# A four-layer linear-attention and PEER kernel: 83 of its 96 sets of five transposes go from TensorE to VectorE and DMAs, and every engine's order is made anew

## The chip, the cores and the metric

The kernel runs on one core of one Trainium2 chip. The metric is device time in microseconds (us) of one execution; lower is better. Before the change three runs took 755.93, 756.91 and 757.05 us, median 756.91 us. All arithmetic is fp32 or built from pairs of the rounded type fp32r, so that products keep nearly fp32 precision.

## The reference, cut to what matters

Two layers, each a linear-attention block A and a product-key expert block B, both with a layer norm in front and a residual behind. 2048 tokens, D = 576, 32 heads of 18.

```python
def A(x, wqkv, wo):                       # H = 32 heads, 18 wide
    q, k, v = split_heads(x @ wqkv)
    phi = lambda t: where(t > 0, t + 1, exp(t)) + 1e-6
    pq, pk = phi(q), phi(k)
    kv = einsum("bhsd,bhse->bhde", pk, v)  # over all 2048 tokens
    z = pk.sum(tokens)
    o = (pq @ kv) / (pq . z + 1e-6)
    return o @ wo

def B(x, w_q, k1, k2, u, v):              # 64 experts = 8 x 8
    q1, q2 = halves(x @ w_q)              # 32 heads, 128 wide each
    i1, i2 = argmax(q1 @ k1.T), argmax(q2 @ k2.T)
    e = i1 * 8 + i2                       # one expert per head
    act = gelu(x . u[e])                  # softmax over one score is 1
    return sum over heads of act * v[e]

x = x + A(layernorm(x));  x = x + B(layernorm(x))
x = x + A(layernorm(x));  x = x + B(layernorm(x))
```

## The kernel before, in words

The 2048 tokens are 16 tiles of 128. For every tile and layer there are three points at which a tile with tokens on its partitions has to become the stationary operand of a product, with channels on its partitions: the normalized input of attention (kind f), the attention output before `wo` (kind o) and the normalized input of the experts (kind b). That is 3 kinds x 16 tiles x 2 layers = 96 sets. Each set is a 128 x 640 tile (576 channels, padded to five blocks of 128). `transposed` (line 190) makes it: five TensorE transposes by the identity into a PSUM tile `pt`; ScalarE copies PSUM to the high part `thi`, rounded to fp32r (line 102); VectorE subtracts it from PSUM for the low part `tlo` (line 103). Products then take 28 matmuls of 288 columns: high by high, high by low, low by high (line 212 for k, v and q; line 402 for `wo`), or 14 of 512 columns for the expert scores (line 433). The small expert-count tile `cg` (128 x 128) is transposed with the kind-b set, where both are ready together, and gets one high and one low copy with it.

The stages run over tiles. In the front of a layer every tile gets its norm, kind f, k and v, and its part of the state `kva` (line 283), which needs all 16 tiles before the layer's back can begin: `state_mask` (VectorE, lines 305 to 308), `state_sum` (the sums `zb`), and five `state_fold` products that multiply the state into `wo`. In the back a tile gets `num` (GpSimd multiplies pq by `zb`, line 371; VectorE sums, inverts and scales, lines 374 to 379), kind o, `ppo`, a residual (line 391), the norm, kind b, the scores, the selection (VectorE, lines 461 to 498), the expert output `po` and the second residual. The front of layer 1 is interleaved with the back of layer 0. The q products of layer 1 for tiles 0 to 12 come late, from high and low parts that `keep` stores to DRAM and `rl` loads into the space of the weights for k and v. While layer 0 begins, 64 slices of `w_q` are folded with the keys (line 550).

The order is written out: each piece (k0.13 is the k product of layer 0, tile 13) is a generator whose steps are played in a listed order, and `in_order` chains the instructions of TensorE, ScalarE, VectorE and GpSimd in that order. All DMAs go through one queue on SyncE (SP). Each DMA waits on SP for its source or its buffer, and everything behind it on SP waits too. The order of SP is left to the framework. Tiles of normalized rows (`y`) have 3 buffers, stationary pairs 4, PSUM tiles 4.

## Time and profile before

| | |
|---|---|
| median of 3 runs | 756.91 us (755.93 to 757.05) |
| span of the profiled execution | 753.7 us |
| time outside that span, against the median | 3.2 us |
| TensorE busy | 736.8 us, 98% |
| VectorE busy | 456.8 us, 61% |
| ScalarE busy | 289.1 us, 38% |
| GpSimd busy | 197.7 us, 26% |
| DMA moved, share of 16 engines | 79.48 MB, 31.8% on the queue that SP issues to |
| granted TensorE clock | 0.998 |

The profiled execution's own time is its span, from the first to the last instruction; the runs' times hold 3.2 us more, which lies outside. Busy time of an engine is the union of its instructions, so instructions that overlap at their ends count once. In a group of instructions the columns are line, engine, operation, out<-in, shapes and count, then busy us and mean ns of one, then idle time ahead of the group and what ended it. In a timeline they are start, duration, engine, line, operation and, in brackets, idle time ahead. Names of tiles: `thif`, `tloo`, `ptb` and the like are the high part, the low part and the PSUM tile of kinds f, o and b; `ppk`, `ppv`, `ppq`, `ppo`, `pps` are products in PSUM.

### The profile page before, as it was taken

To read this page: it belongs to the slowest core of one execution; us is meant where nothing else is said; L and a number is where in the kernel's file an instruction comes from. 1 tells how busy PE (TensorE), PEld (TensorE's weight loads), DVE (VectorE), ACT (ScalarE), POOL (GpSimd) and SP (SyncE) were. 2 spreads that over 40 slices of the span, in tenths; PEclk is the share of its full clock that TensorE was granted. 3 is DMA by queue.
4 is the path that set the end of the run, shared out by engine and by line. 5 is a ranking of instruction groups with operands and counts; after the bars stand their busy time and mean duration, and the time that the engine had idled before them with its cause. 6 is when DMAs were issued, how large, how long until landed. Compare 5 with 4: busy or idle time off the path is not lost.

```text
span 753.7 us, 13987 instructions
## 1 busy us (share of the span) xinstructions
PE 736.8 (98%) x5356; PEld 693.2 (92%) x5356; DVE 456.8 (61%) x1008; ACT 289.1 (38%) x586; POOL 197.7 (26%) x540
## 2 busy tenths in 40 slices
...
GB/s 275 245 125 223 157 171 220 218 118 49 48 63 32 110 89 77 98 84 83 92 105 101 83 67 60 111 68 38 206 107 112 85 65 115 48 48 58 70 33 63
DMA packets 52267, 79.48 MB, mean 105 GB/s; under 512 B 5480, under 2 KB 22376, under 8 KB 52200
## 3 DMA queue, kind: packets, MB, share of 16 engines
q1 hardware_dynamic: 52200, 78.59, 31.8%
q8 instruction: 42, 0.69, 0.4%
...
## 4 chain that ended last, share of the span: by engine, by line
PE 81%; DVE 10%; ACT 3%; issue 2%; POOL 2%; DMA 1%; SPq 0%; DVEq 0%; POOLq 0%; ACTq 0%
PE ppk L212 15%; PE ppv L212 15%; PE ppo L402 13%; PE pps L433 12%; PE ppq L212 11%; PE kva L283 4%; PE fold_ps L550 2%; PE ptf L197 2%; PE ptb L197 2%; PE po L517 2%; PE pto L197 2%; PE m L332 1%; DVE tloo L103 1%; DVE o L379 1%; DVE x L391 1%
## 5 line engine op out<-in xcount | busy, mean ns | idle before, releaser
L219 DVE TENSOR_SCALAR ek<-ek 128x576 f32<-128x576 f32 x32 | 14.7, 459 | 81.4 <-ACT ek L218 76.9
L212 PE MATMUL ppk<-whi,thif 128*128 128x288 f32 x320 | 50.4, 301 | 1.6 <-ACT thif L102 1.6
L402 PE MATMUL ppo<-ohi,thio 126*128 126x288 f32 (+1 forms) x320 | 50.9, 301 | 0.8 <-DVE ct L492 0.5
L212 PEld LDWEIGHTS ppk<-whi,thif 128*128 128x128 f32 x320 | 44.2, 188 | 5.6 <-issue 3.3
L163 POOL TENSOR_SCALAR rsf<-mvf 128x1 f32<-128x1 f32 x16 | 3.1, 192 | 175.6 <-DVE mvf L161 175.4
L212 PE MATMUL ppk<-whi,tlof 128*128 128x288 f32 x320 | 48.7, 296 | 0.3 <-DVE tlof L103 0.3
L212 PE MATMUL ppv<-whi,thif 128*128 128x252 f32 x320 | 48.0, 296 | 0.1
L187 ACT ACTIVATE yb<-x,rsb 128x640 f32<-128x640 f32 x32 | 29.5, 923 | 47.9 <-POOL rsb L180 47.9
L212 PE MATMUL ppv<-whi,tlof 128*128 128x252 f32 x320 | 47.6, 295 | 0.0
L219 DVE TENSOR_SCALAR eq<-eq 128x576 f32<-128x576 f32 x32 | 15.8, 493 | 51.7 <-ACT eq L218 51.7
L433 PE MATMUL pps<-shi,thib 128*128 128x512 f32 x160 | 44.4, 407 | 2.0 <-ACT thib L102 2.0
L402 PEld LDWEIGHTS ppo<-ohi,thio 126*128 126x128 f32 (+1 forms) x320 | 44.6, 189 | 1.9 <-issue 0.7
L212 PEld LDWEIGHTS ppk<-whi,tlof 128*128 128x128 f32 x320 | 44.6, 188 | 0.5 <-DVE tlof L103 0.5
L212 PEld LDWEIGHTS ppv<-whi,tlof 128*128 128x128 f32 x320 | 44.6, 188 | 0.0
L212 PEld LDWEIGHTS ppv<-whi,thif 128*128 128x128 f32 x320 | 44.2, 188 | 0.3 <-ACT thif L102 0.3
L438 ACT ACTIVATE s<-pps 128x512 f32<-128x512 f32 x32 | 19.1, 596 | 61.4 <-PE pps L433 61.4
L433 PE MATMUL pps<-shi,tlob 128*128 128x512 f32 x160 | 42.5, 395 | 0.0
L103 DVE TENSOR_TENSOR tlof<-ptf,thif 128x640 fp32r<-128x640 f32 x32 | 26.2, 818 | 24.3 <-ACT thif L102 24.2
L402 PE MATMUL ppo<-ohi,tloo 126*128 126x288 f32 x256 | 40.3, 295 | 0.0
L402 PE MATMUL ppo<-olo,thio 126*128 126x288 f32 x256 | 40.3, 296 | 0.0
L212 PE MATMUL ppk<-wlo,thif 128*128 128x288 f32 x256 | 39.9, 296 | 0.0
L212 PE MATMUL ppq<-whi 128*128 128x288 f32 x260 | 39.6, 299 | 0.1
...
## 6 DMA issues: line engine op xcount, KB each, us to landing
fold<-in_wq_t SPq DMA_DIRECT2D x64, 288.0 KB, 4.8
whi<-hl_d SPq DMA_DIRECT2D x26, 320.0 KB, 3.5
pq_d<-eq SPq DMA_DIRECT2D x19, 288.0 KB
pq<-pq_d SPq DMA_DIRECT2D x19, 288.0 KB, 3.3
xf<-in_x SPq DMA_DIRECT2D x16, 288.0 KB, 4.7
x<-in_x SPq DMA_DIRECT2D x16, 288.0 KB, 2.8
x_d<-x SPq DMA_DIRECT2D x16, 288.0 KB, 3.1
x<-x_d SPq DMA_DIRECT2D x16, 288.0 KB, 2.6
```

What stands on the lines that cost most here:

```text
L103: eng.tensor_tensor(lo, src, hi.bitcast(F32), op=ALU.subtract)
L187: nc.scalar.activation(y, x2, AF.Identity, scale=rs[:, 0:1], bias=rs[:, 1:2])
L197: nc.tensor.transpose(pt[:, b * P:(b + 1) * P], x, ident)
L212: nc.tensor.matmul(o[:, at:at + c1 - c0], tt[a == "lo"][:, b, :], wb[:, cols + c0:cols + c1], start=(i == 0), stop=(i == len(todo) - 1))
L219: nc.vector.tensor_scalar(e, e, 1.0, EPS, op0=ALU.min, op1=ALU.add)
L283: nc.tensor.matmul(a[:w, c * HC:(c + 1) * HC], vt[:, c * w:(c + 1) * w], fk[:, c * HC:(c + 1) * HC], start=(t == 0 and c == 0), stop=(t == ...
L332: nc.tensor.matmul(m[:c, h * 512:h * 512 + HALF], kvb[:n, b * HC:b * HC + c], wob[l][b][:n, h * HALF:(h + 1) * HALF], start=True, stop=True)
L402: nc.tensor.matmul(p[:, h * 512:h * 512 + HALF], hl[a][:r, b], w[:r, h * HALF:(h + 1) * HALF], start=(i == 0), stop=(i == len(todo) - 1))
L433: nc.tensor.matmul(p[:, :512], hl[a == "lo"][:, b, :], shi[:, b] if w == "hi" else slo[:, blocks(REM)[b][1]], start=(i == 0), stop=(i == l ...
L438: nc.scalar.activation(s[:, NE:], p[:, :512], AF.Copy)
L517: nc.tensor.matmul(p[:, b * 512:b * 512 + HALF], c[i], vmix[:, b * HALF:(b + 1) * HALF], start=(i == 0 and not based), stop=(i == 1))
L550: nc.tensor.matmul(p[32 * j:32 * j + 32, at:at + c1 - c0], kpad[:, ch // 2, 24 - 8 * a:56 - 8 * a], st[:, c0:c1], start=(a == 0), stop=(a ...
```

## The change

- 83 sets leave TensorE. VectorE transposes the tile's 32 x 32 blocks (`qf`, `qo`, `qb`), one DMA writes the result to DRAM (`t_d`), and four DMAs read it back so that the blocks land in place (`rf`, `ro`, `rb`), in runs of 160 elements. ScalarE then makes the high part and another engine the low part, both from SBUF. 13 sets stay on TensorE: kind f of tiles 0 and 1 of both layers and tile 15 of layer 1, kind o of tiles 0 and 1 of layer 0 and 0 of layer 1, kind b of tiles 0 and 1 of both layers and tile 12 of layer 1.
- Of the 83 sets, the 56 of kinds o and b have their low part made by GpSimd, the 27 of kind f by VectorE.
- The 32 transposes of `cg` stay on TensorE, each with a PSUM tile and a pair of its own.
- For the q of layer 1 (16 tiles) phi's VectorE `min` is replaced by two more ScalarE passes (`lean`).
- In the selection three VectorE maxima become one reduction.
- `y`, `q` and `r` tiles share 6 buffers. All pieces have more steps, and one list orders TensorE, ScalarE, VectorE, GpSimd and now SP.

```diff
+YB, TB = 6, 4
+ON_PE = {('f',0,0),('f',0,1),('o',0,0),('b',0,0),('f',1,0),('o',1,0),('b',1,0),('o',0,1),('b',0,1),('f',1,1),('b',1,1),('f',1,15),('b',1,12)}
+KEPT = {(1, t) for t in range(13)}
+LEAN = {1}
+LO_POOL = {("o", 0), ("o", 1), ("b", 0), ("b", 1)}
...
+    def turned(kind, l, t, y, step=P):
+        n = f"{kind}{l}_{t}"
+        if (kind, l, t) in ON_PE:
+            pt = psum(f"pt{n}")
+            for b in range(NB):
+                nc.tensor.transpose(pt[:, b * P:(b + 1) * P], y[:, b * step:b * step + P], ident)
...
+            return hi, lo
+        q = wk.tile([P, NB * P], F32, tag="y", name=f"q{n}", bufs=YB)
+        src = bass.AP(tensor=y.tensor, offset=y.offset, ap=[y.ap[0], [step, NB], [32, 4], [1, 32]])
+        nc.vector.transpose(q.rearrange("p (q b c) -> p b q c", q=4, b=NB), src)
+        yield
+        nc.sync.dma_start(t_d[kind, t], q)
+        yield
+        return (yield from landed(kind, l, t, stationary))
+
+    def landed(kind, l, t, home, who=None):
+        n = f"{kind}{l}_{t}"
+        r = wk.tile([P, NB * P], F32, tag="y", name=f"r{n}", bufs=YB)
+        w = 32 * NB
+        for a in range(4):
+            nc.sync.dma_start(r[32 * a:32 * a + 32].rearrange("r (i e) -> r i e", i=4),
+                              t_d[kind, t][:, a * w:(a + 1) * w].rearrange("(i r) e -> r i e", i=4))
+        yield
+        hi, lo = home(n)
+        src = r.rearrange("p (i b c) -> p b i c", i=4, b=NB)
+        h, l4 = (x.rearrange("p b (i c) -> p b i c", i=4) for x in (hi, lo))
+        nc.scalar.activation(h, src, AF.Copy)
+        yield
+        (nc.gpsimd if (who or kind, l) in LO_POOL or (who or kind, l, t) in LO_POOL else nc.vector).tensor_tensor(l4, src, h.bitcast(F32), op=ALU.subtract)
         return hi, lo
...
+        if lean:
+            nc.scalar.activation(e2, halves(p), AF.Relu, scale=-1.0)
+            nc.scalar.activation(e, e, AF.Exp, scale=-1.0)
+            nc.scalar.activation(e, e, AF.Identity, bias=small[:, 0:1])
+        else:
+            nc.scalar.activation(e2, halves(p), AF.Exp)
+        yield
+        if not lean:
+            nc.vector.tensor_scalar(e, e, 1.0, EPS, op0=ALU.min, op1=ALU.add)
         nc.vector.scalar_tensor_tensor(e2, halves(p), 0.0, e2, op0=ALU.max, op1=ALU.add)
...
-        nc.vector.tensor_tensor(mt, s[:, :256], s[:, 256:512], op=ALU.max)
-        nc.vector.tensor_tensor(mt[:, :128], mt[:, :128], mt[:, 128:], op=ALU.max)
...
-        nc.vector.tensor_tensor(mx, mt[:, :64], mt[:, 64:128], op=ALU.max)
+        nc.vector.tensor_reduce(mx, sv.rearrange("p e g -> p g e"), axis=AX.X, op=ALU.max)
...
+    with in_order(*ALL, ET.SP):
...
+            lq1.12 sel1.7 O1.15 bT1.8 gel1.7 cT1.5 sel1.7 oT1.9 num1.11 gel1.7 oT1.10 cT1.5 oT1.9 sel1.7 po1.5 lq1.12 S1.8 sel1.7
...
```

TensorE in the back of layer 1, where tile 8 comes to its scores (`po` is the expert output, `pc` the transposed `cg`). Before:

```order
L197 MATMUL pto_10_8106<-ident,o_10_7832 128x128 x5
L197 MATMUL ptb_8_8134<-ident,yb_8_8118 128x128 x5
L197 MATMUL ptb_8_8134<-ident,cg_6_8061 128x128
L402 MATMUL ppo_9_8156<-ohi,thio_9_7953 128x288 x10
L402 MATMUL ppo_9_8156<-olo,thio_9_7953 128x288 x8
L402 MATMUL ppo_9_8156<-ohi,tloo_9_7954 128x288 x8
L402 MATMUL ppo_9_8156<-olo,tloo_9_7954 128x288 x2
L433 MATMUL pps_8_8185<-shi,thib_8_8141 128x512 x5
L433 MATMUL pps_8_8185<-slo,thib_8_8141 128x512 x4
L433 MATMUL pps_8_8185<-shi,tlob_8_8142 128x512 x5
```

and now:

```order
L455 MATMUL pc_5_8621<-ident,cg_5_8558 128x128
L233 MATMUL ppq_12_8628<-whi 128x288 x10
L233 MATMUL ppq_12_8628<-wlo,whi 128x288 x8
L233 MATMUL ppq_12_8628<-whi 128x288 x10
L554 MATMUL po_5_8694<-vmix,chi_5_8665 128x288 x2
L554 MATMUL po_5_8694<-vmix,clo_5_8666 128x288 x2
L473 MATMUL pps_8_8703<-shi,thib_8_8623 128x512 x5
L473 MATMUL pps_8_8703<-slo,thib_8_8623 128x512 x4
L473 MATMUL pps_8_8703<-shi,tlob_8_8624 128x512 x5
```

The two sets of five transposes are gone from this place; the scores of tile 8 stand behind the q of tile 12 and the expert output of tile 5.

SP at the same place. Before, only loads of rows and stores of the output:

```order
L532 DMA out<-x_4_7907 128x576
L354 DMA x_11_7867<-x_d_146 128x576
L532 DMA out<-x_5_8047 128x576
L354 DMA x_10_7889<-x_d_145 128x576
L532 DMA out<-x_6_8275 128x576
```

and now:

```order
L205 DMA t_db_189<-qb_7_8308 128x640
L215 DMA rb_7_8372<-t_db_189 32x4x160 x4
L205 DMA t_do_175<-qo_9_8378 128x640
L389 DMA x_15_8415<-x_d_149 128x576
L569 DMA out<-x_13_7967 128x576
L215 DMA ro_9_8476<-t_do_175 32x4x160 x4
L569 DMA out<-x_6_8468 128x576
L205 DMA t_db_190<-qb_8_8501 128x640
L215 DMA rb_8_8565<-t_db_190 32x4x160 x4
L569 DMA out<-x_14_8585 128x576
```

A write and its four reads stand next to one another, or with one or two other DMAs between.

GpSimd at the same place (`g` is the gelu, `rsb` the norm's factors, line 406 multiplies pq by `zb`). Now:

```order
L487 TENSOR_SCALAR g_7_8619<-g_7_8619 128x64
L488 TENSOR_TENSOR g_7_8619<-g_7_8619,s_7_8407 128x64
L223 TENSOR_TENSOR tlob_8_8624<-rb_8_8565,thib_8_8623 128x640
L418 COPY o_11_8590<-o_11_8590 128x56
L492 TENSOR_SCALAR g_7_8619<-g_7_8619 128x64
L493 TENSOR_TENSOR g_7_8619<-g_7_8619,s_7_8407 128x64
L223 TENSOR_TENSOR tloo_9_8676<-ro_9_8476,thio_9_8675 128x640
L424 CAST tloo_9_8676<-thio_9_8675 16x128
L406 TENSOR_TENSOR o_12_8733<-eq_12_8699,zb 128x576
L223 TENSOR_TENSOR tloo_10_8729<-ro_10_8681,thio_10_8728 128x640
```

Lines 223 are the low parts that VectorE made on line 103 before; they now stand between the short steps of gelu and norm.

More of the change, by code (lines that the diff above doesn't have):

```diff
@@ L79, in network @@
     nc.gpsimd.memset(mhalf, -0.5)
+    small = cp.tile([P, 1], F32, name="small")
+    nc.gpsimd.memset(small, EPS)
     kpad = cp.tile([P, 2, 56], F32, name="kpad")
@@ L133, in split_weight, with weight @@
-    def split_weight(tiles, c0, hi, lo, rem, which=range(NB), eng=nc.vector):
-        for b in which:
-            cols = slice(c0, c0 + D)
-            if b != rem:
-                split(tiles[b], hi[:, b, cols], lo[:, blocks(rem)[b][1], cols], eng)
-            else:
-                split_mixed(tiles[b], hi[:, b, cols])
+    def weight(c, b):
+        r, bl = blocks(REM)[b]
+        cols = slice((1, 2, 0)[c] * D, (1, 2, 0)[c] * D + D)
+        st = stage(f"wst{c}_{b}", NB * c + b)
+        if b != REM:
+            nc.sync.dma_start(st, wqkv[r:r + P, cols])
+        else:
+            nc.sync.dma_start(st[:64], wqkv[r:r + 64, cols])
+            nc.sync.dma_start(st[64:], wqkv[r:r + 64, cols])
+        yield
+        hi = whi[:, b, cols]
+        nc.scalar.activation(hi, st, AF.Copy)
+        yield
+        if b != REM:
+            (nc.gpsimd if (c, b) == (0, 3) else nc.vector).tensor_tensor(wlo[:, bl, cols], st, hi.bitcast(F32), op=ALU.subtract)
+        else:
+            nc.vector.tensor_tensor(hi[64:], st[64:], hi[64:].bitcast(F32), op=ALU.subtract)
@@ L188, in normalized, with stationary @@
         return y.rearrange("p a b -> p (a b)")
[L190 to L202 removed]
+    def stationary(n):
+        return tuple(wk.tile([P, NB, P], F32R, tag=a, name=f"{a}{n}", bufs=TB) for a in ("thi", "tlo"))
@@ L231, in front_T @@
     def front_T(l, t):
-        tt["f", l, t] = yield from transposed(ys.pop(("f", l, t)), f"f{l}_{t}")
+        tt["f", l, t] = yield from turned("f", l, t, ys.pop(("f", l, t)))
     def front_k(l, t):
```

445 lines of the change are left out of this document (215 added, 230 removed).

## The prediction

> **What bounds the kernel now.** First the page's busy time, then who TensorE (PE) waits for.
>
> ```profile
> PE 736.8 (98%) x5356; PEld 693.2 (92%) x5356; DVE 456.8 (61%) x1008; ACT 289.1 (38%) x586; POOL 197.7 (26%) x540
> PE ptb L197 <- DVE cg L498: 3.1, 2, 2.3
> ```
>
> TensorE is busy for 98% of the span; its longest group of waits is 3.1 us. So work taken from it shortens the kernel, if nothing else becomes late. Whether it does is a matter of stages. The table of busy time by windows (after the window: PE, PEld, DVE, ACT, POOL, clock, DMA share, GB/s) shows the last stage, from the end of layer 1's state:
>
> ```profile
> 535.00:560.00 25.00, 24.62 (x173) 23.34 (x172) 15.65 (x29) 7.44 (x12) 7.01 (x9) 1.00 0.47 128
> 560.00:580.00 20.00, 19.66 (x143) 18.95 (x142) 10.14 (x18) 8.62 (x14) 5.82 (x15) 1.00 0.36 103
> 620.00:640.00 20.00, 19.49 (x138) 18.41 (x138) 19.31 (x41) 7.49 (x14) 7.23 (x19) 1.00 0.34 108
> 740.00:753.70 13.70, 6.42 (x30) 4.69 (x29) 8.40 (x27) 3.40 (x8) 1.42 (x4) 0.87 0.22 86
> sum 218.70, PE 208.39 PEld 192.66 DVE 178.75 ACT 82.72 POOL 79.06; mean PE 18.94 PEld 17.52 DVE 16.25 ACT 7.52 POOL 7.19
> ```
>
> There VectorE (DVE) is nearly full too: 178.8 us of 218.7, and 19.3 of 20 between 620 and 640. It is the second bound, in this stage alone.
>
> **What a set costs TensorE.** The timeline of TensorE in a steady step, and one set with a product behind it:
>
> ```profile
> 372.15 1.49 PE L212 MATMUL ppv<-whi,tlof 128*128 128x252 f32 x10
> 373.48 0.71 PE L197 MATMUL ptb<-ident,yb 128*128 128x128 f32 x5
> 374.02 0.27 PE L197 MATMUL ptb<-ident,cg 128*128 128x128 f32 x1
> 374.13 0.71 PE L197 MATMUL ptf<-ident,yf 128*128 128x128 f32 x5
> 374.68 1.05 PE L283 MATMUL kva<-ek,v 128*127 128x126 f32 x8
> 458.69 0.71 PE L197 MATMUL pto<-ident,o 128*128 128x128 f32 x5
> 459.15 1.58 PE L212 MATMUL ppk<-whi,thif 128*128 128x288 f32 x10
> 460.57 1.23 PE L212 MATMUL ppk<-wlo,thif 128*128 128x288 f32 x8
> L197 PE MATMUL ptb<-ident,yb 128*128 128x128 f32 x160 | 22.8, 273 | 0.6 <-ACT yb L187 0.6
> ```
>
> The second number, 0.71 us, is from the first start to the last end, and the last 0.16 us lie under what follows. What counts is start to start: 0.54 us (373.48 to 374.02) and 0.55 (374.13 to 374.68). At 458.69 only 0.46 pass, but the ten matmuls behind then take 1.42 to the next start where ten usually take 1.33 (372.15 to 373.48): 0.55 again. I take 0.545 us, five times 0.109. 83 x 0.545 = **45.2 us less**. Bounds: 83 x 0.46 = 38.2 and, by the busy time, 83 x 0.71 = 58.9. The `cg` transposes and all products stay.
>
> The row's mean for one transpose is 273 ns. The Trainium skill, TensorE: Matmul & The Clock Gate, Part 4: PE-mode transpose, gives about 275 ns for one in a kernel; the row agrees as a duration. By that figure as a slot the sets would be worth 83 x 5 x 0.275 = 114 us, an estimate from that page. The starts say 0.109.
>
> **What VectorE, GpSimd and ScalarE get.** No row shows a VectorE transpose.
>
> ```profile
> L468 DVE TENSOR_TENSOR m<-s,mx x32: 691/692/846, 258.8 to 743.8; 128x512 bf16<-128x512 f32 x32
> L379 DVE TENSOR_TENSOR o<-pq,r x19: 757/758/1752, 235.7 to 704.1; 128x576 f32<-128x576 f32 x19
> L103 DVE TENSOR_TENSOR tlof<-ptf,thif x32: 811/815/826, 9.7 to 519.2; 128x640 fp32r<-128x640 f32 x32
> L219 DVE TENSOR_SCALAR eq<-eq 128x576 f32<-128x576 f32 x32 | 15.8, 493 | 51.7 <-ACT eq L218 51.7
> L462 DVE TENSOR_TENSOR mt<-mt 128x128 f32<-128x128 f32 x32 | 9.4, 293 | 1.1
> L464 DVE TENSOR_TENSOR mx<-mt 128x64 f32<-128x64 f32 x32 | 7.3, 227 | 1.1
> L489 DVE TENSOR_REDUCE pi<-pr 128x16 int32<-128x512 bf16 x32 | 21.9, 686 | 1.1
> L461 DVE TENSOR_TENSOR mt<-s 128x256 f32<-128x256 f32 x32 | 16.3, 511 | 4.4 <-ACT s L438 4.4
> L461 DVE TENSOR_TENSOR mt<-s x32: 412/419/1526, 257.7 to 742.8; 128x256 f32<-128x256 f32 x32
> L187 ACT ACTIVATE yb<-x,rsb 128x640 f32<-128x640 f32 x32 | 29.5, 923 | 47.9 <-POOL rsb L180 47.9
> ```
>
> 512 and 576 columns take 0.692 and 0.758: 1.03 ns a column, so 640 take 0.82, as line 103 does. A one-operand pass (L219, 0.49 for 576) would give 0.55: the lower bound; 0.84 (0.758 x 640/576) the upper. I take 0.82.
>
> Last stage, VectorE: 28 sets (15 o, 13 b) bring 28 x 0.82 = +23.0 and lose as many low parts, 28 x 0.82 = -23.0. Thirteen late q lose the `min`, 13 x 0.49 = -6.4; three q go ahead of the stage, each with the `min` and one pass of 576 like line 379's, -3 x (0.49 + 0.76) = -3.8. Sixteen selections: 0.511 + 0.293 + 0.227 against 0.69 for one reduction, -5.5. The count tile's low part becomes an instruction of its own, at the fixed share of the two rows (0.692 - 512 x 1.03 ns = 0.16): 16 x 0.16 = +2.6. Together -13.1.
>
> Against it stands a cost that the trace shows. The timelines of GpSimd and VectorE (POOL rows from one, DVE rows from the other):
>
> ```profile
> 640.35 1.42 POOL L371 TENSOR_TENSOR o<-pq,zb 128x576 f32<-128x576 f32 x1
> 640.60 1.31 DVE L482 TENSOR_TENSOR oh<-cd,code_w 128x256 bf16<-128x256 bf16 x1
> 647.75 0.69 DVE L468 TENSOR_TENSOR m<-s,mx 128x512 bf16<-128x512 f32 x1
> 647.76 1.99 POOL L371 TENSOR_TENSOR o<-eq,zb 128x576 f32<-128x576 f32 x1
> 657.64 0.29 DVE L482 TENSOR_TENSOR oh<-cd,code_w 128x256 bf16<-128x256 bf16 x1
> L498 DVE TENSOR_TENSOR cg<-g,c 128x128 f32<-128x128 f32 x32 | 11.5, 358 | 3.9 <-POOL rsb L178 0.9
> L498 DVE TENSOR_TENSOR cg<-g,c x32: 291/292/1368, 264.2 to 747.8; 128x128 f32<-128x128 f32 x32
> ```
>
> An `oh` that takes 0.29 takes 1.31 when it starts inside a long GpSimd multiplication, and ends with it; at 647.75 the other way round, the multiplication takes 1.99. The Trainium skill, SBUF — State Buffer, Who interferes with whom, says that GpSimd and a VectorE instruction with two SBUF inputs lock each other out for a whole instruction; the trace agrees (1.31 against 0.29), and the page speaks against 56 more such GpSimd instructions. What it costs here: L461's mean is 92 ns over its median and L498's 66, so 32 x 0.158 = 5.1 us over 32 multiplications, 0.16 each. Other groups have such tails; I take 0.27, and bounds 0 and 1.0 (1.31 - 0.29). A low part on GpSimd is 1.42 x 640/576 = 1.58 us. So 28 x 0.27 = +7.6 in the last stage.
>
> VectorE there: 178.8 - 13.1 + 7.6 = 173.3 us. TensorE: 208.4 - 28 x 0.545 - 3 x 3.73 (the three q moved ahead, 28 matmuls each at 0.133) = 181.9, and with its 10.3 idle 192.2. VectorE goes from 86% to 95% of TensorE's work. In the window at 620 with VectorE at 96.6% TensorE lost 0.5 of 20 us. For the whole stage, 2.5% of 182: **+4.6 us**. Bounds: 0; and VectorE with the 40 us of idle that it has there now, 173.3 + 40.0 = 213.3, which is +21.1.
>
> In the earlier stages VectorE is far from full. ScalarE gets 32 more passes of at most 0.92 (L187), GpSimd 56 x 1.58 = 88 us; in the last stage that makes at most 83 + 24 and 79 + 44 of 192, all beside TensorE's work. What is queued behind such a subtraction on GpSimd is a short step of norm or gelu; if no other tile's work covers it, each costs TensorE up to 1.58.
>
> **The way through DRAM.** Issues and landing times, and the queue's share:
>
> ```profile
> 375.89 0.32 SPq L259 DMA_DIRECT2D hl_d<-thif  x1
> hl_d<-tlof SPq DMA_DIRECT2D x13, 320.0 KB, 3.2
> wst<-in_wqkv SPq DMA_DIRECT2D x12, 288.0 KB, 5.5
> q1 hardware_dynamic: 52200, 78.59, 31.8%
> 9.55 0.53 PE L212 MATMUL ppk<-whi,thif 128*128 128x288 f32 x2 [0.81 <-ACT thif L102]
> 26.00 1.44 SPq L589 DMA_DIRECT2D xf<-in_x  x2
> ```
>
> A set now takes 0.82 (transpose), 0.33 and 3.2 (write), 4 x 0.33 and 3.2 (reads), at most 0.92 (high part, as L187) and 0.82 or 1.58: some 11 us, against 2.3 before (0.55, 0.92, 0.82). With sixteen tiles in flight other work covers it; a set whose cover is gone would cost up to 9 us. Bytes: 83 x 2 x 0.328 MB = 54.4 MB more on 78.6, so the share goes from 32 to 54%: no bound.
>
> The cover is thinnest at the start. TensorE begins at 9.55 and has six products (28 matmuls at 0.133 each, 22.4 us), two state parts (a little over the 1.05 of line 283 each) and eleven fold steps, about 26 us, before the first turned tile's q: until 35.5. That tile's write is the 38th DMA on SP; before, the 36th and 37th went out at 26.0. So it goes at about 28, and the tile is ready at 28 + 3.2 + 1.3 + 3.2 + 1.7 = 37 or, with 5.5 to land, at 42: **+4 us**, bounds 0 and 8.
>
> **The sum.** The profiled execution: 753.7 - 45.2 + 4 + 4.6 = 717.1. The median of the runs is 3.2 above its span (756.9 against 753.7): 720.3, say **720 us**. Bounds: 753.7 - 58.9 + 3.2 = 698 and 753.7 - 38.2 + 8 + 21.1 + 3.2 = 747.8.
>
> **The rivals.**
>
> *GpSimd's subtractions stop VectorE.* Each of the 28 in the last stage catches a two-input VectorE instruction and holds it 1.0 us: 165.7 + 28 = 193.7, plus the idle that the stage's beginning and end force (9.4 + 9.9 + 5.3 in the windows at 535, 560 and 740): 218, as long as before. The rest gains 45.2 - 15.3 - 11.2 - 4 = 14.7: 739 + 3.2 = 742. For it: the rows at 640 and 647. Against: means near the medians. Chance 0.11.
>
> *SP becomes the bound, and the kernel slower.* Where a write and its reads stand side by side, everything behind waits on SP: 0.33 + L + 4 x 0.33 for a set, with L the landing. The middle stage begins with TensorE's first sums `z`:
>
> ```profile
> 229.15 1.13 PE L314 MATMUL z<-kvb,pick 127*128 127x126 f32 x8 [0.48 <-DVE kvb L305]
> ```
>
> From there to 535, 306 us, it has 41 sets and about 105 other DMAs, the last 28 and 56. At L = 3.2 that is 199 + 35 and 136 + 18: room. SP decides from 69 x (1.65 + L) + 53 = 306 + 218.7, L = 5.2; the kernel is slower than before from 5.3, with the 7.6 us that the first stage's 14 sets give. At `wst`'s 5.5: 493 + 53 = 546, +21.7 - 7.6 = +14, 768 + 3 = 771. For it: that row, and the doubled share. Against: landing is 3.2 where the share is about 0.3, and some pairs have other work between. Chance 0.11.
>
> *A set is worth its whole busy time, and nothing new waits:* 698. Against: the starts above. Chance 0.04. *Each transpose frees its whole 273 ns:* 83 x 5 x 0.273 = 113 less, 753.7 - 113 + 8.6 + 3.2 = 652. Chance 0.01, since the starts exclude it. The figure of the Trainium skill's Part 4 above, read as a slot, is this case.
>
> **How the numbers follow.** The forecast has 0.73, own range 706 to 736. A measurement of this kernel tells about 0.2% from no change. Of the first rival 0.02 reach up to or past the old time. Faster: 0.73 + 0.09 + 0.05 = 0.87; within 0.2%: 0.02; slower: 0.11. The range 703 to 748 leaves out the SP case, the two small ones and the top of the first: 0.18.
>
> **What would show it.** TensorE busy near 736.8 - 83 x 0.71 = 678; each transpose on VectorE 0.82; GpSimd near 286 with rows of 1.58 at line 223; two-input rows of VectorE with longer tails; the write landing near 3.2. Wrong if TensorE's waits in the last stage are on high or low parts whose reads landed late (SP), or if VectorE is full there and TensorE well below 95%.

## The result: 3.1% slower, and the profile after

| | before | after |
|---|---|---|
| median of the runs | 756.91 us (755.93 to 757.49, 5 runs) | 780.81 us (775.38 to 781.36, 5 runs) |
| span of the profiled execution | 753.7 us | 773.6 us |
| granted clock | 0.998 | 0.978 |

The ratio is 1.031, 95% interval [1.028, 1.034]. The forecast was 720 us with a range to 748. The profile after is that of the run of 775.38 us; the other four took 780.50 to 781.36.

First the busy times of the page after, then the windows of the three stages (cut at layer 0's and layer 1's state sums), of before and of after: PE, PEld, DVE, ACT, POOL, clock, DMA share, GB/s.

```profile
PE 724.8 (94%) x4941; PEld 663.1 (86%) x4941; DVE 502.0 (65%) x982; ACT 319.1 (41%) x645; POOL 299.7 (39%) x597
```

```profile
0.00:229.20 229.20, 224.66 (x1821) 210.70 (x1821) 82.90 (x168) 73.82 (x160) 20.94 (x60) 1.00 0.47 157
229.20:536.60 307.40, 304.93 (x2170) 290.93 (x2171) 196.40 (x440) 132.58 (x269) 97.67 (x272) 1.00 0.27 88
536.60:753.70 217.10, 207.17 (x1369) 191.59 (x1367) 177.54 (x402) 82.72 (x157) 79.06 (x208) 0.99 0.24 75
```

```profile
0.00:236.00 236.00, 229.85 (x1702) 204.54 (x1703) 92.52 (x182) 75.27 (x159) 22.67 (x61) 0.99 0.60 189
236.00:561.60 325.60, 309.67 (x2126) 294.23 (x2125) 226.98 (x438) 146.03 (x298) 149.83 (x300) 0.98 0.55 174
561.60:773.60 212.00, 185.28 (x1117) 164.36 (x1115) 182.49 (x364) 97.82 (x188) 127.17 (x236) 0.96 0.51 154
```

TensorE has 415 matmuls less, yet is busy only 12.0 us less, not 59 as forecast. The first stage grew by 6.8 us, the middle one by 18.2, and the last shrank by 5.1. The new order also moves q products, 28 matmuls or 3.73 us each: the stages had 392, 84 and 420 matmuls into `ppq` before and have 336, 252 and 308 after, so two products left the first stage, four (not three) the last, and six came to the middle one. By 0.545 us a set (14, 41 and 28 sets), 3.73 a product and 15.3 for the fold steps (below), an estimate, the stages should have changed by +0.2, 0 and -30.2 us. They are 6.6, 18.2 and 25.1 us over that, so the last stage lost most. TensorE's idle time went from 16.9 us (753.7 - 736.8) to 48.8. Three things are new: the price of the fold steps, the waits, and the clock.

**The fold steps.** The groups of the fold's matmuls, of before and of after:

```profile
L550 PE MATMUL fold_ps<-fold,kpad 128*32 128x320 f32 (+1 forms) x256 | 17.5, 410 | 0.0
```

```profile
L587 PE MATMUL fold_ps<-fold,kpad 128*32 128x256 f32 (+1 forms) x256 | 32.8, 411 | 0.0
```

The same 256 matmuls take 15.3 us more. The timelines of TensorE (start, duration) show how, first before, then after:

```profile
64.78 2.19 PE L550 MATMUL fold_ps<-fold,kpad 128*32 128x320 f32 x32
66.90 1.60 PE L212 MATMUL ppk<-whi,thif 128*128 128x288 f32 x10
```

```profile
29.43 1.16 PE L587 MATMUL fold_ps<-fold,kpad 128*32 128x320 f32 x4
30.51 1.15 PE L317 MATMUL kva<-ek,v 128*127 128x126 f32 x8
40.30 6.11 PE L587 MATMUL fold_ps<-fold,kpad 128*32 128x320 f32 x40
46.34 0.93 PE L233 MATMUL ppq<-whi,thif 128*128 128x288 f32 x5
```

A fold step is `fold_mm(m)`: four matmuls (as the trace counts them) into the 32 columns of group m mod 4. Before, eight steps with the groups in turn 0 1 2 3 0 1 2 3 took 2.12 us. After, one step alone takes 1.08, and ten steps take 6.04: their groups, from the order list, are 3 1 1 1 2 2 2 0 0 3. Counting a new round wherever a group comes again gives 2 rounds before (1.06 us each), 1 and 6 after (1.08, and 1.01 each).

**The waits.** TensorE's longest groups after (total, times, longest; before, the first was 3.1 and the second 2.0):

```profile
PE pc L455 <- DVE cg L535: 12.9, 9, 3.8
PE pps L473 <- ACT thib L221: 4.7, 3, 2.4
PE po L554 <- DVE clo L460: 4.2, 5, 1.4
PE kva L317 <- DVE ek L249: 3.6, 2, 3.4
```

Three of the four end with VectorE. Only one ends with a part that came through DRAM; two smaller groups do too, `pps` after `tlob` (2.0) and `ppo` after `tloo` (0.4), both made by GpSimd.

**The clock.** TensorE after a cluster of waits:

```profile
274.59 0.33 PE L455 MATMUL pc<-ident,cg 128*128 128x128 f32 x1 [2.17 <-DVE cg L535]
277.39 2.60 PE L440 MATMUL ppo<-ohi,thio 126*128 126x288 f32 x10
279.79 2.12 PE L440 MATMUL ppo<-olo,thio 126*128 126x288 f32 x8
```

Ten such matmuls usually take 1.49 or 1.50 us and eight 1.23. Here they take 2.60 and 2.12. Windows of 1 us show the granted clock itself: 1.00 up to 275, 0.71 in the next, 0.50 from 276 to 282, 0.88, and 1.00 again from 283. Over the span the clock is 0.978, which is, as an estimate, 773.6 x 0.022 = 17.0 us of missing speed against 753.7 x 0.002 = 1.5.

So the span's +19.9 us is, roughly, -45.2 (the sets) + 15.3 (folds) + 31.9 (idle) + 15.5 (clock) = +17.5. The remaining 2.4 us are not assigned.

**What VectorE and GpSimd paid.** The new rows, and two rows of the selection with two SBUF inputs each (before: L468 mean 704, L473 mean 447 ns):

```profile
L203 DVE STREAM_TRANSPOSE qo<-o 128x640 f32<-128x640 f32 x29 | 24.1, 833 | 3.0 <-POOL o L418 2.9
L223 POOL TENSOR_TENSOR tlob<-rb,thib 128x640 fp32r<-128x640 f32 x27 | 44.1, 1633 | 12.1 <-ACT thib L221 10.2 <-PE ppo L440 0.7 <-issue 0.4
L501 DVE TENSOR_REDUCE mx<-s 128x64 f32<-128x512 f32 x32 | 34.2, 1070 | 9.5 <-ACT s L476 9.5
L504 DVE TENSOR_TENSOR m<-s,mx 128x512 bf16<-128x512 f32 x32 | 31.1, 973 | 1.1
L509 DVE SCALAR_TENSOR_TENSOR m<-m 128x256 bf16<-128x256 bf16 x32 | 20.0, 625 | 0.5
```

The durations of the row of line 504, shortest, median and longest:

```profile
L504 DVE TENSOR_TENSOR m<-s,mx x32: 691/693/2012, 269.9 to 762.4; 128x512 bf16<-128x512 f32 x32
```

The transpose costs what was forecast (0.82). The reduction does not (0.69). The `m` row's median is unchanged at 693 ns, but its mean is 280 ns above that and its maximum 2012. What holds such instructions is in the timeline:

```profile
311.33 1.99 POOL L223 TENSOR_TENSOR tloo<-ro,thio 128x640 fp32r<-128x640 f32 x1 [0.26 <-DMA ro<-t_do]
311.94 1.67 DVE L509 SCALAR_TENSOR_TENSOR m<-m 128x256 bf16<-128x256 bf16 x1
320.23 2.07 PE L317 MATMUL kva<-ek,v 128*127 128x126 f32 x8 [3.35 <-DVE ek L249]
```

An instruction of 0.45 us takes 1.67. From 316.9 on TensorE waits 3.35 us for VectorE and then runs at half rate (2.07 where 1.05 to 1.15 is usual, at a granted clock of 0.50 from 320 to 323).

### The profile page after: what moved, and what is told of

It reads as the page before. It is cut to its first block, busy times and chain, and to the rows that moved or that the text cites. A ratio compares the mean times of both kernels' runs of the same rounds, so it can differ in the third digit from the quotient of the medians.

```text
span 773.6 us, 14064 instructions
## 1 busy us (share of the span) xinstructions
PE 724.8 (94%) x4941; PEld 663.1 (86%) x4941; DVE 502.0 (65%) x982; ACT 319.1 (41%) x645; POOL 299.7 (39%) x597
## 4 chain that ended last, share of the span: by engine, by line
PE 56%; DVE 22%; DMA 6%; POOL 6%; issue 5%; ACT 3%; SPq 2%; DVEq 0%; POOLq 0%; ACTq 0%
PE ppk L233 12%; PE ppv L233 12%; PE ppq L233 12%; PE pps L473 4%; PE ppo L440 4%; PE fold_ps L587 4%; PE kva L317 3%; DVE mx L501 2%; DVE m L504 2%; DVE x L429 2%; DMA pq<-pq_d 2%; DMA ro<-t_do 2%; DVE m L509 1%; DVE pi L525 1%; DVE pr L521 1%
## 5 line engine op out<-in xcount | busy, mean ns | idle before, releaser
L406 POOL TENSOR_TENSOR o<-pq,zb 128x576 f32<-128x576 f32 x19 | 27.4, 1444 | 132.1 <-ACT zb L351 124.2
L223 POOL TENSOR_TENSOR tloo<-ro,thio 128x640 fp32r<-128x640 f32 x29 | 46.8, 1615 | 11.6 <-ACT thio L221 10.7
L473 PE MATMUL pps<-shi,thib 128*128 128x512 f32 x160 | 43.8, 403 | 7.9 <-ACT thib L221 4.7
L223 POOL TENSOR_TENSOR tlob<-rb,thib 128x640 fp32r<-128x640 f32 x27 | 44.1, 1633 | 12.1 <-ACT thib L221 10.2
L406 POOL TENSOR_TENSOR o<-eq,zb 128x576 f32<-128x576 f32 x13 | 19.1, 1475 | 76.2 <-ACT zb L351 61.9
L273 ACT ACTIVATE v<-ppv 128x252 f32<-128x252 f32 x64 | 21.4, 378 | 66.1 <-PE ppv L233 58.5
L223 DVE TENSOR_TENSOR tlof<-rf,thif 128x640 fp32r<-128x640 f32 x27 | 22.0, 815 | 40.6 <-PE ppq L233 11.3
L473 PE MATMUL pps<-shi,tlob 128*128 128x512 f32 x160 | 44.6, 411 | 2.0 <-POOL tlob L223 2.0
L168 ACT ACTIVATE junk<-x,mb 128x576 bf16<-128x576 f32 x32 | 24.8, 774 | 51.8 <-POOL mb L166 51.4
L245 ACT ACTIVATE ek<-ppk 128x576 f32<-128x576 f32 x32 | 20.8, 651 | 60.5 <-PE ppk L233 60.5
L249 DVE SCALAR_TENSOR_TENSOR eq<-ppq,eq 128x576 f32<-128x576 f32 x32 | 24.1, 755 | 30.0 <-ACT eq L243 28.8
```

What stands on the lines that cost most here:

```text
L168: nc.scalar.activation(junk, xt, AF.Square, bias=m[:, 0:1], accum_out=m[:, 1:2])
L223: (nc.gpsimd if (who or kind, l) in LO_POOL or (who or kind, l, t) in LO_POOL else nc.vector).tensor_tensor(l4, src, h.bitcast(F32), op=AL ...
L245: nc.scalar.activation(e2, halves(p), AF.Exp)
L249: nc.vector.scalar_tensor_tensor(e2, halves(p), 0.0, e2, op0=ALU.max, op1=ALU.add)
L273: nc.scalar.activation(vt[:, c * w:(c + 2) * w].rearrange("p (c e) -> p c e", c=2)[:, :, :HC], x.rearrange("p (c e) -> p c e", c=2), AF.Copy)
L406: nc.gpsimd.tensor_tensor(o[:, :D], pq, zb, op=ALU.mult)
```

## The experiments

Times are medians; a ratio is to the kernel before. After stands at 780.8, before at 756 to 757 in every comparison.

### Parts of the changed kernel undone

**e1: the fold steps of each lot take the column groups in turn.** Ten steps in the list, for example (the other pieces between them are left out here):

```diff
- F0.3 F0.1 F0.5 F0.9 F0.2 F0.6 F0.10 F0.4 F0.8 F0.7
+ F0.1 F0.2 F0.3 F0.4 F0.5 F0.6 F0.7 F0.8 F0.9 F0.10
```

> The changed kernel with one thing undone: inside each unbroken batch of fold matmuls on TensorE (line 587), the slices are put in an order in which the four column groups of 32 take turns, as they did before the change; everything else, the other engines' orders too, stays. Fold theory: the changed list put matmuls of one column group behind one another, and the fold matmuls went from 22.5 us busy to 40.4; with turns they come back to about 24, the first stage ends some 15 us earlier, and the time falls from about 780 to 762 to 768. Rival (the fold matmuls are dearer because they stand in small batches or wait for their slices): busy stays above 36 and the time within 4 us of the change's.

775.9 us, ratio 1.025 [1.022, 1.028]. The lot of ten fell from 6.04 to 3.05 us, three rounds for 1 2 3 0 1 2 3 0 1 2:

```profile
40.71 3.13 PE L587 MATMUL fold_ps<-fold,kpad 128*32 128x320 f32 x40
43.76 1.46 PE L233 MATMUL ppq<-whi,thif 128*128 128x288 f32 x9
```

But a step that stands alone still takes its 1.08, and there are many. The row of line 587 falls from 32.8 to 28.2 us, so the gain of 4.9 us is about what the row lost. Both expectations missed: the theory had about 24 us of fold work and 762 to 768, the rival more than 36 and a change within 4 us.

**e2: all low parts on VectorE.**

```diff
- LO_POOL = {("o", 0), ("o", 1), ("b", 0), ("b", 1)}
+ LO_POOL = set()
```

> The changed kernel with all 83 low parts made by VectorE, none by GpSimd; the orders stay. Lock theory (GpSimd's 1.6 us subtractions hold VectorE's instructions with two SBUF inputs): the means of those rows come back to their medians (the mask of line 504 from 973 to about 710 ns, line 509 from 625 to about 440), VectorE's busy time rises by less than the 46 us that 56 subtractions of 0.82 cost, to about 515 to 520 from 502, TensorE waits less, and the time falls by 3 to 15 us. Rival (VectorE is simply full in the middle and last stage): its busy time rises by about 46 us, and the time rises by 10 to 25 us.

772.2 us, 1.020 [1.017, 1.022], so 8.6 us faster than the change. The page's busy times, and the two rows, which are nearly back to before:

```profile
PE 722.1 (94%) x4941; PEld 660.1 (86%) x4941; DVE 510.2 (67%) x1038; ACT 319.2 (42%) x645; POOL 211.9 (28%) x541
```

```profile
L504 DVE TENSOR_TENSOR m<-s,mx 128x512 bf16<-128x512 f32 x32 | 24.0, 751 | 1.1
L509 DVE SCALAR_TENSOR_TENSOR m<-m 128x256 bf16<-128x256 bf16 x32 | 14.1, 441 | 0.2
```

VectorE took over 56 instructions of 0.82 us, 45.9 us, and is busy only 8.2 us more. The other 37.7 us had been time in which its instructions were held: 0.67 us for each subtraction on GpSimd, where the forecast had 0.27. Work moved off VectorE cost it nearly as much as it had before. That an instruction with two SBUF inputs is held until a GpSimd instruction that reads SBUF and came first has ended is what the Trainium skill, SBUF — State Buffer, Who interferes with whom, states; the trace agrees (1.67 against 0.45, with GpSimd's instruction ending at 313.32). In the profiles e2 gains in the middle stage, 319.5 us against 325.6; the last stage stays at 211.9 against 212.0.

**e3: three maxima in place of the one reduction.**

```diff
- nc.vector.tensor_reduce(mx, sv.rearrange("p e g -> p g e"), axis=AX.X, op=ALU.max)
+ nc.vector.tensor_tensor(mt, s[:, :256], s[:, 256:512], op=ALU.max)
+ nc.vector.tensor_tensor(mt[:, :128], mt[:, :128], mt[:, 128:], op=ALU.max)
+ nc.vector.tensor_tensor(mx, mt[:, :64], mt[:, 64:128], op=ALU.max)
```

> The changed kernel with the three maxima of before in place of the one reduction of line 501, which takes 1070 ns. Forecast's price (0.69 for the reduction) would make this slower by some us; by the rows the three maxima take 0.94 at their medians, but two-input instructions can be held by GpSimd: the theory that the reduction only lost its gain, and is not what makes the kernel slower than before, expects the time within 4 us of the change's. Rival (the reduction's 0.38 us on the way from the scores to the expert output is what TensorE waits for): 8 us or more faster.

783.2 us, 1.035 [1.033, 1.037]. In this kernel the three take 0.520, 0.479 and 0.343 us, 1.34 together, more than the reduction's 1.07: they are two-input instructions and are held as well. The interval overlaps the change's [1.028, 1.034], so the two are not told apart. Whether a reduction at the forecast's 0.69 would have helped is not shown: this edit put a longer way in its place.

**e4: the 27 sets of kind b back on TensorE,** their transposes at the place of the high part.

```diff
+ if kind in BACK:                       # BACK = "b"
+     pt = psum(f"pt{n}")
+     for b in range(NB):
+         nc.tensor.transpose(pt[:, b * P:(b + 1) * P], y[:, b * step:b * step + P], ident)
+     ...                                # high and low part from PSUM
```

> The changed kernel with all kind-b sets on TensorE again (40 sets on TensorE, 56 through DRAM): the transposes and the high part stand where the high part stood, the low part (VectorE, from PSUM) where it stood on GpSimd; orders otherwise the same. It takes 27 writes, 108 reads and 27 GpSimd subtractions away and adds 27 x 0.545 = 14.7 us to TensorE. Theory that late parts and held VectorE instructions cost more than the transposes: GpSimd busy falls by 44 us, TensorE's waits fall by more than 15 us, the time falls by 2 to 12 us. Rival (TensorE's own work sets the time): 10 to 15 us slower.

804.7 us, 1.063 [1.060, 1.066], 23.9 more than the change and beyond both expectations. TensorE is busy 18 us more and waits besides, 7.8 us on `tlob`. So in this order TensorE's transposes cost more than their own time where they now have to stand. Kinds f and o were not tried.

**e6: no transposes on VectorE; e7: reads that wait for no write; e8: a second write.** The three ask what of a set's new way costs time.

```diff
# e6: the untransposed tile is written
- nc.vector.transpose(q.rearrange("p (q b c) -> p b q c", q=4, b=NB), src)
- nc.sync.dma_start(t_d[kind, t], q)
+ nc.sync.dma_start(t_d[kind, t].rearrange("p (b c) -> p b c", b=NB), src)
# e7: the reads come from an input
- t_d[kind, t][:, a * w:(a + 1) * w]
+ bass.AP(tensor=x_in.tensor, offset=t * P * D // 2 + a * w, ap=[[NB * P, P], [1, w]])
# e8
+ nc.sync.dma_start(t_d2[kind, t], q)
```

> The changed kernel without the 83 transposes of VectorE: the untransposed tile is written to DRAM instead, so that the sums are others and every later step, DMA and product stays. It leaves out 83 x 0.83 = 69 us of VectorE, 40 of them in layer 0's selections. Theory that VectorE's own load makes TensorE wait: TensorE's idle falls from 49 us to 30 or less and the time from 781 to 758-768. Theory that the length of the way through DRAM makes it wait: 0.83 us of some 11 go, the time stays within 4 us of 781.

> The changed kernel with the four reads of a set taken from an input tensor of the same size instead of what the set has just written; the write stays, the numbers are others. The reads wait for no landing any more (3 to 4 us of the way of each set, and as long on SP). Theory of the length of the way through DRAM, or of SP held by it: the time falls by 10 us or more, to 771 or less, and the waits of TensorE on high parts go. Theory of VectorE's load: within 4 us of 781.

> The changed kernel with every set written to DRAM a second time, to a place that nobody reads: 83 DMAs and 27 MB more on SP's queue. If SP or the DMA engines set the pace (the prediction's rival), each costs its issue and the longer queue, 0.4 us or more, 83 x 0.4 = 33 us: 800 or more. If they do not: within 4 us of 781.

e6: 766.1 us (1.012 [1.009, 1.015]), 14.7 less than the change. e7: 779.2 (1.030 [1.027, 1.033]), 1.6 less, which is not told apart from the change. e8: 786.8 (1.040 [1.037, 1.043]), 6.0 more, 0.07 us for each extra DMA with the queue's share at 63.0%, between its two expectations. So of the three VectorE's own 69 us count most, and the landing of the DMAs and SP little. But they are not the whole loss: TensorE's idle falls only from 48.8 to 40.2 us, where 30 or less was expected. And the gain lies in the middle stage alone. The windows of e6 for the middle and the last stage:

```profile
235.90:550.70 314.80, 305.92 (x2125) 291.58 (x2124) 197.03 (x396) 146.00 (x298) 148.63 (x300) 0.99 0.58 180
550.70:763.10 212.40, 185.94 (x1117) 165.99 (x1116) 167.63 (x337) 97.29 (x188) 127.11 (x236) 0.96 0.53 154
```

The middle stage has 314.8 us against 325.6. The last has 212.4 against 212.0, though VectorE has 14.9 us less to do there. In the windows of 20 us after, VectorE stands at up to 18 of 20 in the middle stage, and TensorE loses up to 4 us:

```profile
260.00:280.00 20.00, 15.96 (x82) 13.53 (x81) 17.65 (x33) 8.55 (x16) 12.93 (x24) 0.89 0.54 166
340.00:360.00 20.00, 18.05 (x116) 16.34 (x115) 18.01 (x33) 8.98 (x21) 14.66 (x27) 1.00 0.50 152
520.00:540.00 20.00, 20.00 (x153) 20.00 (x152) 4.41 (x7) 3.73 (x8) 0.00 (x0) 1.00 0.12 48
```

From 500 to 560 VectorE has almost nothing. The new order does the middle stage's selections first and leaves plain products for its end.

**e9: the 64 fold steps in 17 lots,** nearly all of four steps with four groups. **e10: these lots, the low parts of e2, and ten more warm-up matmuls. e11: e10 without those warm-ups, and without VectorE's transposes as in e6.**

```diff
# e9, in the list: taken out where they stood, and put in together
+ ... F0.0 F0.1 F0.2 F0.3 ... F0.4 F0.5 F0.6 F0.7 ... F0.8 F0.9 F0.10 ... F0.11 F0.12 F0.13 F0.14 ...
# e10, besides
- wu0.2
+ wu0.9
- fT0.0 wk0.0 wv0.1
+ fT0.0 wu0.3 wk0.0 wv0.1
```

> The changed kernel with its 64 fold steps gathered into 17 lots, nearly all of four steps with four different column groups, each placed where its data are due; nothing else is moved. Theory that a lot costs 1.06 us for each step that its fullest column group has (from the runs so far: 1.08 for one step, 1.12 for four of different groups, 2.12 for eight, 6.04 for ten with four in one group): the fold work of the first stage goes from 32.6 us to 17-19, and the time from 781 to 764-769. Rival, that their order hardly matters beyond the 5 us that the first try gave: 774 or more.

> The changed kernel with three things mended together: the lots of the run named e9, all low parts on VectorE, and ten more warm-up matmuls ahead of the first product (the first ten products' matmuls run at half rate). If the losses are separate and add: 781 - 14 - 9 - 2 = 756, the time of the kernel before; if the gain in the first stage is lost in waits later: above 762.

> The run named e10 without the ten warm-up matmuls and without the 83 transposes of VectorE (the untransposed tile goes through DRAM, so the sums are others). It is the floor of the change if VectorE's turning cost nothing. If the three losses (lots, lock, VectorE's load) are separate: 781 - 14 - 9 - 15 = 743; the rest to the forecast of 720 is then the order of the selections. If the lock and the load are the same loss (VectorE's time), 752 or more.

e9: 774.6 us (1.022 [1.019, 1.025]), 6.2 less than the change; the rival's number. A lot of four now takes 1.13 us, and the fold row falls to 23.2 us. But in the first stage TensorE is busy 4.9 us less than in e1 and idle 4.9 us more (1.0 of it for a fold's load, the rest for ScalarE, VectorE and a high part), so that e1 and e9 end that stage together. e10: 763.0 (1.009 [1.007, 1.011]), 17.8 less than the change, still above before, and by its expectation a case of gains lost again in later waits (above 762). e11: 749.9 (0.991 [0.989, 0.993]), between its two expectations. So folds, lock and start together are 18 us and VectorE's turning another 13. Some 30 us above the forecast are left even with all of it gone.

### The kernel before, with one thing done to it

**e5: the fold steps sorted by column group.**

```diff
- for m in groups:
+ for m in sorted(groups, key=lambda m: (m % 4, m)):
```

> The kernel before, with the fold steps of each tile step sorted so that two of the same column group stand side by side; the same 256 matmuls. Theory that neighbours of one column group cannot overlap (0.15 us from start to start where 0.07 is usual): half of the 256 stand behind one of their own group, so the fold rows go from 17.5 us busy to about 28, and the kernel from 756 to 764-768. Rival, that the fold steps are dear in the changed kernel only because they stand in small lots among other work: busy stays below 20 and the time within 2 us of 756.

779.9 us, 1.031 [1.030, 1.033]: this line alone costs as much as the whole change. Groups 0 0 1 1 2 2 3 3 make five rounds:

```profile
68.24 5.13 PE L550 MATMUL fold_ps<-fold,kpad 128*32 128x320 f32 x32
73.30 1.60 PE L212 MATMUL ppk<-whi,thif 128*128 128x288 f32 x10
```

5.06 us where two rounds take 2.12, eight times: 23.5 us of the 23.4 measured. I had expected half that, since I took the loss by neighbours and not by rounds.

**e12: ten sets of layer 0's front turned by VectorE,** in the old order.

```diff
# in the tile loop of the first stage, tiles 4 to 13
+ turn_in(t + 1)                         # four reads, at the start of a step
  ...
+ first_ln(0, t + 2)                     # the norm a step earlier
+ turn_out(t + 2)                        # VectorE transposes, one write
  ...
+ turn_split(t + 1)                      # high part ScalarE, low part VectorE
- run(0, (q, t), (fT, t + 1), (st, t))
+ run(0, (q, t), (st, t))
```

> The kernel before, with its own order, in which only the sets of tiles 4 to 13 of layer 0's first stage go the new way: VectorE transposes, one write, four reads; the high and low parts stay with ScalarE and VectorE. There VectorE is busy for a third, TensorE never waits, and a tile has a whole step of some 15 us for the way. Theory that a set is worth 0.545 us to TensorE wherever its way is covered, and that the change loses elsewhere: 10 x 0.545 = 5.5, 756.6 - 5.5 = 751 (750 to 752). Rival, that the way through DRAM costs TensorE time by itself (late tiles, a lower granted clock): 755 or more. Rival, that a set is worth its busy time of 0.71: 749.5.

750.0 us, 0.992 [0.991, 0.993], 6.4 less than before (between 5.1 and 7.1 by the interval), and the span 5.4 less. The state sum of layer 0, of before (already shown at 229.15) and here, and that of layer 1 in both:

```profile
223.18 1.13 PE L339 MATMUL z<-kvb,pick 127*128 127x126 f32 x8 [0.47 <-DVE kvb L330]
529.61 1.16 PE L339 MATMUL z<-kvb,pick 127*128 127x126 f32 x8 [0.38 <-DVE kvb L330]
```

```profile
535.69 1.16 PE L314 MATMUL z<-kvb,pick 127*128 127x126 f32 x8 [0.38 <-DVE kvb L305]
```

229.15 - 223.18 = 5.97 us for ten sets, 0.60 each, and the middle stage is as long as before (306.4 against 306.5). The price of a set holds where VectorE is free and the way has a whole step of time. (The edit also gives these tiles a fourth buffer and puts the loads of rows ahead of the fold's; what that does by itself is not shown.) The times alone give 0.51 to 0.71 us a set, so they do not tell 0.545 from the rival's 0.71; the state sums lie between the two.

**e13: eight more sets, in the middle stage.**

```diff
# in step2, layer 1's tiles 3 to 10
+ turn_out(s - 2, 1)
- run(1, (v, s - 3), (fT, s - 2), (keep, s - 2 if s - 2 < 13 else -1), (st, s - 3))
+ run(1, (v, s - 3), (st, s - 3))
  ...
+ turn_in(s - 2, 1)
  run(0, (gel, s), (sel, s, 2), (po, s - 1), (O, s + 1), (sel, s))
+ turn_split(s - 2, 1)
+ run(1, (keep, s - 2))
```

> The kernel named e12 with eight more sets the new way, tiles 3 to 10 of layer 1's front, which lie in the middle stage beside layer 0's selections; the old order stays (within a step: VectorE transposes and the write early, the reads in the middle, the parts at the end). VectorE is busy there for 13 to 17 of 20 us before, and gets 0.83 a step more. Theory that the sets pay in the old order in the middle stage too, and that the changed kernel's own order (selections packed until VectorE is full) is what costs it there: 8 x 0.545 = 4.4, 750.0 - 4.4 = 745.7 (744.5 to 747). Rival, that a set beside the selections costs what it gains, whatever the order: 749 or more.

809.2 us, 1.069 [1.068, 1.071]: 59 us lost with eight sets, 7.4 each, far beyond both expectations. The timeline where one step begins, ScalarE and TensorE:

```profile
350.05 0.92 ACT L188 ACTIVATE yf<-x,rsf 128x640 f32<-128x640 f32 x1 [1.99 <-POOL rsf L181]
353.76 0.72 ACT L255 ACTIVATE thif<-rf 128x640 fp32r<-128x640 f32 x1
354.54 2.77 PE L213 MATMUL ppk<-whi,thif 128*128 128x288 f32 x10 [5.38 <-ACT thif L255]
357.10 2.12 PE L213 MATMUL ppk<-wlo,thif 128*128 128x288 f32 x8
359.02 2.10 PE L213 MATMUL ppk<-whi,tlof 128*128 128x288 f32 x10
360.96 1.49 PE L213 MATMUL ppv<-whi,thif 128*128 128x252 f32 x10
```

TensorE waits 5.38 us for a high part that stands on ScalarE behind the next tile's normalizations (`yf` above, then `yb`): my placement, as e14 shows, not the DMA. And the wait is not its whole price. The 28 matmuls that follow take 6.4 us, from 354.54 to 360.96, where 28 take 3.73. The Trainium skill, TensorE: Matmul & The Clock Gate, Part 1: The HAM clock gate, says that the array falls to half its clock after some 3.4 us of idleness and rises again after as long. This trace agrees on the fall: the granted clock, in windows of 1 us, is 1.00 up to 353, some 4 us into the wait, 0.78 in the next and 0.50 from 354 to 360, and the 28 matmuls cost 2.7 us more. Full speed came back later than by the page's figure, in the window from 360 to 361, some 6 us after work began. And in the kernel after no single wait of that length was needed: the clock fell in the window from 275 to 276, after waits of 2.17 and 0.37 us with one matmul of 0.33 between them.

**e14: the parts ahead of those normalizations.**

```diff
- run(0, (gel, s), (sel, s, 2), (po, s - 1), (O, s + 1), (sel, s))
- turn_split(s - 2, 1)
- run(1, (keep, s - 2))
- run(0, (ld, s + 3))
+ run(0, (gel, s), (sel, s, 2))
+ turn_split(s - 2, 1)
+ run(1, (keep, s - 2))
+ run(0, (po, s - 1), (O, s + 1), (sel, s), (ld, s + 3))
```

> The kernel named e13 with one thing moved: in each of the eight steps the high and low part of the turned tile stand on ScalarE and VectorE ahead of the last pieces of the step before's output, instead of behind them. In e13 TensorE waited 5.4 us in each of the eight steps for a high part that stood behind two normalizations on ScalarE, not for a DMA, and its next products then ran at half rate (2.77 us for ten matmuls in place of 1.49). Theory that this place was the loss and that a set pays beside the selections in the old order: 745.7 (744.5 to 747.5). Rival, that the reads land too late for the step or hold ScalarE: 752 or more, with the waits of TensorE on the high part still there.

751.1 us, 0.993 [0.992, 0.994]: the 58 us are back, but the eight sets give nothing beyond e12, neither the 745.7 of the theory nor the 752 of the rival. A step from product to product, here and then in the kernel before:

```profile
342.39:360.12 17.73, 17.66 (x125) 16.53 (x123) 12.11 (x28) 8.07 (x16) 6.87 (x18) 1.00 0.39 125
```

```profile
348.25:366.04 17.79, 17.79 (x131) 17.12 (x129) 11.63 (x27) 7.90 (x16) 5.91 (x18) 1.00 0.26 88
```

It is 0.06 us shorter (the next one 0.13), not 0.545. VectorE has 12 of 17.7 us, so it is not full. The state step shows where the rest is:

```profile
350.48 1.14 PE L308 MATMUL kva<-ek,v 128*127 128x126 f32 x8
350.68 0.81 ACT L103 ACTIVATE thib<-ptb 128x768 fp32r<-128x768 f32 x1
351.39 0.23 ACT L273 ACTIVATE v<-ppv 128x72 f32<-128x72 f32 x1
351.67 0.21 PEld L310 LDWEIGHTS kva<-ek,v 128*73 128x73 f32 x2 [0.24 <-ACT v L273]
```

It waits for ScalarE's copy of v. Before, the five transposes stood in front of the state step and covered that copy.

**e15: that copy ahead of the high part.**

```diff
- run(1, (v, s - 3, 1))
+ run(1, (v, s - 3))
  run(0, (bc, (s, s - 1)))
- run(1, (v, s - 3), (st, s - 3))
+ run(1, (st, s - 3))
```

> The kernel named e14 with one instruction moved: ScalarE's copy of the last 72 columns of the value product stands ahead of the high part of the next set instead of behind it. In e14 a step takes 17.69 us from product to product where the kernel before takes 17.78, 0.09 less instead of 0.545: TensorE's state step now waits for that copy (0.24 us, and 1.19 to the next start where 0.89 is usual), which the five transposes covered before. Theory that the transposes taken away were the cover of another wait, so that a set pays only where what it covered is moved too: a step falls by another 0.3 to 0.45, 8 x 0.3 to 0.45 = 2.4 to 3.6, 751.1 to 747.5-748.7. Rival, that the step is bound elsewhere: 750.5 or more.

748.4 us, 0.989 [0.987, 0.991], as the theory had it, and the fastest kernel of this study: 8.5 us under before. The two state sums stand at

```profile
223.38 1.13 PE L339 MATMUL z<-kvb,pick 127*128 127x126 f32 x8 [0.47 <-DVE kvb L330]
527.49 1.16 PE L339 MATMUL z<-kvb,pick 127*128 127x126 f32 x8 [0.38 <-DVE kvb L330]
```

so the middle stage took 304.1 us, 2.4 less than the 306.5 of before, 0.3 for each of the eight sets.

## Why the prediction was wrong

- **The price of a set, 83 x 0.545 = 45.2.** Right as a price where nothing else hangs on it (e12: 0.60 by the state sum). Wrong as a sum over all sets. It takes TensorE's time as free once the transposes are gone; e14 shows it given back to a wait that they had covered, and e15 gets 0.3 a set back by moving what is waited for.
- **"The `cg` transposes and all products stay."** They stay in number, not in cost. I read the order of all engines for the sets only and did not look at the fold steps: +15.3 us of TensorE's busy time, a term that the sum lacked. e5 shows the mechanism by itself. In the changed kernel less of it came back: 4.9 us in e1, 6.2 in e9.
- **"I take 0.27" for a GpSimd subtraction.** It is 0.67 (e2), within the bounds 0 to 1.0 that I gave. I took it from the means of two rows beside 32 multiplications, when VectorE had gaps. The first rival, "GpSimd's subtractions stop VectorE", had the mechanism; undoing it gives 8.6 us, so it is a part of the loss, not the loss.
- **"In the earlier stages VectorE is far from full."** This step failed in the middle stage. It used the old order's windows for a new order. VectorE went to 17 and 18 of 20 us there, and taking its transposes away gives 14.7 us (e6; in the profiles 10.5, all of it in this stage).
- **"For the whole stage, 2.5% of 182: +4.6 us."** This step, for the last stage, failed most. The stage shrank by 5.1 us where the terms asked for 15.3 + 11.2 - 4.6 = 21.9, and a fourth q product, which I had not counted, left it besides. VectorE's load came near the forecast (182.5 us beside TensorE's 185.3, as against 173.3 beside 181.9), but TensorE was idle for 26.7 us there, not 10.3 + 4.6, and its clock was 0.96. The step took VectorE's load for what TensorE would wait for. Without VectorE's transposes the stage is as long (e6: 212.4 us), and without subtractions on GpSimd too (e2: 211.9); without both it has 206.7 (e11). What else holds TensorE there stays open; the named waits are on steps of the selection, of the norm and on high parts.
- **One reduction at 0.69.** It measured 1.07. The row that I took it from reads neighbouring bf16 elements; this one reads fp32 at a stride of 64. Whether that matters for the time is not shown (e3).
- **The clock.** No term for it. The waits shown above were followed by matmuls at about half rate; by the mean clock that is some 15.5 us, an estimate.
- **"A set whose cover is gone would cost up to 9 us."** The size came out near (e13: 7.4), but by luck: in e13 the time went to ScalarE's order and the clock, not to DRAM.
- **The start, +4.** It did not come as a wait: in the first stage TensorE was idle 6.2 us, 1.6 more than before (4.5).
- **SP as the bound.** It rightly had a low chance: reads that wait for nothing gain 1.6 us, and 83 more DMAs cost 6.0. That this rival's 771 is nearer to the time than the forecast is luck; the time came by another way. The DMA share, 54% by forecast, was 55%; the transpose 0.83 against 0.82; the low part 1.62 on GpSimd against 1.58.
- **What would have shown it wrong** named high and low parts landing late in the last stage, and VectorE full there with TensorE well below 95%. Of the second, TensorE's share came true (87%); VectorE had 86% of the stage, up to 19.4 of 20 us in single windows. Of the first, TensorE waited there 5.6 us for such parts (3.9, 1.3 and 0.4); how much of that goes back to the reads is not shown.

Not settled: with folds, lock, start and VectorE's turning taken out, e11 is still 30 us above the forecast. Its profile says where they lie. Its span of 749.8 us is 32.7 above the forecast's 717.1: its fold row is 7.0 us above before's (24.5 against 17.5), TensorE is idle 38.2 us where the forecast has 16.9 + 4 + 4.6, which is 12.7 more, and its clock of 0.980 means some 13.5 us more missing speed than before (an estimate), 33.2 together. What causes that idle time in the new order is not shown. I take it to be the packed order of the selections and waits that the transposes had covered; e14 and e15 show that such waits exist in the old order, but nothing here measured them in the new one.
